# Gate sums in PSUM, bound operands on GpSimd, mask rows by DMA, and a new set of order keys

## The chip, the core and the metric

The kernel runs on one core of a Trainium2 chip. A core has a matrix engine (PE, or TensorE), a vector engine (DVE, or VectorE), a scalar engine (ACT, or ScalarE), GpSimd (POOL), and SyncE (SP), which here only issues transfers. They share an on-chip memory, SBUF; matmul results land in PSUM, eight banks of 512 float32 columns by 128 partitions. Each engine runs its own instructions in program order and waits on semaphores for the others. The metric is the device time in microseconds.

## The reference

The inputs are q, k and v for 4 batches of 8 heads, 768 positions, 64 numbers each, and three weights.

First comes an attention that selects keys. Keys are cut into 24 chunks of 32. For every query and chunk an upper bound of the dot product is formed from the chunk's smallest and largest key in each dimension:

```
ub = sum over d of max(q * k_min, q * k_max)
```

Of the chunks not in the future, the six with the largest bound are kept; scores outside them, or later than the query, are set to -1e9; softmax and the product with v follow.

Then the heads are put side by side (512 channels, x), and a gated unit follows: a causal convolution of five taps along the sequence for each channel, a sigmoid of it as the gate, `val = x @ w_val`, and `out = (gate * val) @ w_out`.

## The kernel before

**Tiling.** Heads are taken in 16 pairs, so that 128 partitions hold two heads of 64 dimensions. A pair passes through four steps, and the steps of neighbouring pairs overlap:

1. `kq`: loads of k, q and v (three buffers each) are issued on SP. PE transposes k and q into PSUM (L524), ScalarE copies them out (L535, L557) and makes a clipped copy of q (L562). VectorE reduces the keys to the largest and smallest of each chunk (L541), and `bounds` turns these into the operand KB by one subtraction of 128x24 (L574) and two of 64x48 (L581). GpSimd writes the float16 operands: KE from k (L549), QU from q (L568), VA from v (L603).
2. `sel`: PE forms the bounds in float32 (L631). VectorE adds the causal fill (L638), finds the eight largest of each row (L647) and writes NS, a one for each chunk that isn't selected (L654). PE transposes NS (L664), and 24 rows of the result are copied into the spare partitions of QU for each head: VectorE does it for the first head, ScalarE for the second (L678). The rows meet a constant of -240 in KE, so the score matmul itself adds the mask.
3. `attn`: score matmuls (L751) into eleven banks per pair, exponentials on ScalarE (L758), triangular cuts on GpSimd (L765), products with v (L782) that also give the row sums, then a reciprocal (L708) and a multiplication (L712) on VectorE. A transposing DMA (L724) writes the result into xT, where channels are on partitions.
4. `moe_gate`: the five taps of a channel tile. The first `taps` of them (`PTAPS`) are matmuls with diagonal matrices, a high and a low float16 part each (L825); the diagonals are built on VectorE in `moe_diag` (L915). The rest are multiply-adds on VectorE (L802): one for each half of the sequence, from PSUM into the float32 SBUF tile g, and then, in place in g, the others over all 768 columns. Tanh follows over 768 columns (L813). For the last two tiles of the last batch PE takes three and five taps, and all goes by halves.

When four pairs (a batch) are through, `moe_val` (L858) and its multiplication with the gate (L865), and `moe_out` (L874, copied out at L880 or L884 and stored at L887) follow.

**What sets the order.** Nothing is issued at once. Each step is added to a `Plan` with an engine, a key, a cost and the names that it reads and writes. `Plan.order` then runs a list schedule: for each engine it takes, of the operations that could start earliest, the one with the smallest key, and allots the PSUM banks under the limits `CAPS` ("w": 4 for transposes, bounds, gates and the rest, "s": 4 for scores, "av": 2). A key is the pair's number plus a small offset, for instance `p + 0.1` for `sel(p + 1)`. Where PE would rest, the planner puts in filler matmuls on zeros (L506); a block of these (L483, L506) also opens the program. The instructions on each engine follow that list, so on SP a load, a transposing DMA and a store stand in one queue.

Of the kernel before, what the change touches and what calls it, by code (L numbers as in the profile page):

```python
# [10 lines left out]
F16 = mybir.dt.float16  # L11
AF = mybir.ActivationFunctionType
# [3 lines left out]

class Op:
    __slots__ = ("eng", "key", "cost", "fn", "kind", "reads", "writes", "new", "need", "ndep",
                 "outs", "after", "ready", "end", "num", "seen")


class Plan:
# [8 lines left out]

    NBANK = 8

    def __init__(self):
        self.ops = []
        self.writer = {}
        self.readers = {}
        self.maker = {}

    def add(self, eng, key, cost, fn, r=(), w=(), new=(), kind=None, at=0.0):  # L40
        o = Op()
        o.eng, o.key, o.cost, o.fn, o.kind, o.new = eng, key, cost, fn, kind, new
# [34 lines left out]
    def order(self, bufs, caps, filler):  # L77

        users, tags, used = {}, {}, {}
        made = {}
        banks = [None] * self.NBANK
# [204 lines left out]
def kernel(  # L288
# [33 lines left out]
    X0 = XP - (KSZ - 1)  # L322
    MASKS = ("DVE", "ACT")

    PTAPS = {(b, ct): 1 + ct % 2 for b in range(B) for ct in range(NCT)}
    PTAPS[B - 1, NCT - 2] = 3
    PTAPS[B - 1, NCT - 1] = 5
    DTAPS = [max(PTAPS[b, ct] for b in range(B)) for ct in range(NCT)]
# [6 lines left out]
    for it in range(1, NT):  # L335
        for p in range(128):
# [8 lines left out]
    BUFS = {"kn": 3, "qn": 3, "vn": 3, "P5": 2, "kmx": 2, "kmr": 2,  # L345
            "q32": 2, "k32": 2, "rq": 2, "mub": 2, "top8": 2, "onat": 2, "rcp": 2, "osb": 4}
    for bi in range(11):
        BUFS[f"P{bi}"] = 2
    for ct in range(NCT):
# [25 lines left out]

    PB = [ps.tile([128, 512], FP, tag=f"bank{i}", name=f"bank{i}") for i in range(Plan.NBANK)]

    plan = Plan()
    T = {}
    new_tile = {}  # L380

# [133 lines left out]
    def kq(p, key):  # L515
# [55 lines left out]

        def bounds(ws, k0):
            c0, c1 = 12 * ws[0], 12 * ws[-1] + 12
            dve(k0, 0.2 if len(ws) > 1 else 0.16, lambda: nc.vector.tensor_tensor(  # L574
                out=T["kmr", p][:, 0, c0:c1], in0=T["kmx", p][:, c0:c1],
                in1=T["kmr", p][:, 1, c0:c1], op=ALU.subtract),
                r=[("kmx", p), ("kmr", p)] + [(x, p, w) for x in ("kmx", "kmn") for w in ws],
                w=[("kmrr", p, w) for w in ws], kind="2")
            for hh in range(2):
                hp, b0 = HP[hh], CC[hh] * NCH  # L580
                dve(k0, 0.33 if len(ws) > 1 else 0.25, lambda hp=hp, b0=b0: nc.vector.tensor_tensor(  # L581
                    out=kb[hp, :, b0 + c0:b0 + c1], in0=T["kmr", p][hp, :, c0:c1],
                    in1=T["kmr", p][hp, :, 0:1].to_broadcast([64, 2, c1 - c0]),
                    op=ALU.subtract),
                    r=[("kmr", p), ("KB", i2), ("kmrr", p, 0), ("kmn", p, 0)]
                    + [("kmrr", p, w) for w in ws],
                    w=[("KBh", i2, hh, w) for w in ws], kind="2")

        if p == 0:
            khalf(0, key)  # L590
# [25 lines left out]
    def part(p, key, g, its, nch, kb, qu, ns, iN, i2):  # L616
# [57 lines left out]
                dve(key, 0.14 + n * 0.072, lambda: fn(copy=nc.vector.tensor_copy), r, w)  # L674

        ws = (g,) if len(its) < SELT else (0, 1)
        for hh in range(2):
            mask(key + 0.35, hh, lambda hh=hh, copy=None: copy(  # L678
                out=qu[CP[hh], hh, its[0] * 128:its[0] * 128 + n * 128],
                in_=T[pt][CP[hh], :]),  # L680
                r=[pt] + [(pt, i) for i in range(n)], w=[("QM", iN, hh, w) for w in ws])
# [14 lines left out]
    def attn(p, key):  # L696
# [98 lines left out]
    def moe_gate(b, ct, key):  # L795
        slot = (b % 2) * NCT + ct
        g, taps = ("g", b, ct), PTAPS[b, ct]
        late = b == B - 1 and ct >= NCT - 2

        def tap(ki, c0, n, dst, src, k0, r, w):  # L800
            i = ki * NCT + ct
            dve(k0, 0.13 + n / 910, lambda: nc.vector.scalar_tensor_tensor(  # L802
                out=dst(), in0=xT[:, slot, X0 + c0 + ki:X0 + c0 + ki + n], scalar=cwT[:, i:i + 1],
                in1=src(), op0=ALU.mult, op1=ALU.add), r=r, w=w,
                new=new(g, f"g{ct}", [128, S]) if ki == taps and c0 == 0 else (),
                kind=None if ki == taps else "2")
            plan.also((g,))

        def half(w):
            return T[g][:, w * HB:(w + 1) * HB]  # L810

        def tanh(k0, n, dst, src, r, w, nw=()):
            act(k0, 0.11 + n / 1220, lambda: nc.scalar.activation(  # L813
                out=dst(), in_=src(), func=AF.Tanh, scale=0.5), r=r, w=w, new=nw)
            plan.also((g,))


        for w in range(2):
            pg = ("pg", b, ct, w)
            rx = [("xT", slot, x) for x in range(w + 1)]  # L820
            n = 0
            for ki in range(taps):
                for hl in range(2):
                    pe(key + 0.1 * w, HB, lambda ki=ki, hl=hl, n=n, w=w, pg=pg:
                       nc.tensor.matmul(  # L825
                           out=T[pg], lhsT=diag[ct][:, ki, hl, :],
                           rhs=xT[:, slot, X0 + w * HB + ki:X0 + w * HB + ki + HB],
# [4 lines left out]
            if taps == KSZ:  # L832
                tanh(key + 0.1 * w, HB, lambda w=w: half(w), lambda pg=pg: T[pg],
                     (pg, (pg, "o")), ((g, "t", w),),
                     new(g, f"g{ct}", [128, S]) if w == 0 else ())
                continue
            tap(taps, w * HB, HB, lambda w=w: half(w), lambda pg=pg: T[pg], key + 0.1 * w,
                rx + [pg, (pg, "o"), "cwT"], ((g, w),))
            if late:
                for ki in range(taps + 1, KSZ):  # L840
                    tap(ki, w * HB, HB, lambda w=w: half(w), lambda w=w: half(w),
                        key + 0.15 + 0.1 * w, rx + ["cwT"], ((g, w),))
                tanh(key + 0.2 + 0.1 * w, HB, lambda w=w: half(w), lambda w=w: half(w),
                     ((g, w),), ((g, "t", w),))
        if not late and taps < KSZ:
            rx = [("xT", slot, x) for x in range(2)]
            for ki in range(taps + 1, KSZ):
# [148 lines left out]
```

## Time and profile before

| | |
|---|---|
| median of three runs | 217.6 us (217.26 to 220.84) |
| the profiled execution | 219.25 us, span 217.5 us |
| PE busy | 199.2 us |
| VectorE busy | 178.0 us |
| ScalarE busy | 159.2 us |
| GpSimd busy | 135.7 us |
| DMA moved | 29.86 MB, mean 137 GB/s |

The span is the time from the first to the last instruction on the core. A group of instructions is given as: line, engine, operation, output and input, shapes, count, then busy time in us, mean duration of one in ns, and the idle time just in front of them with what ended it. Busy time joins overlapping instructions, so it can be less than count times mean. A matmul's duration includes its latency; the chain of work that ended last shows the smaller distance at which they follow each other. Waits are given as the waiting line, what it waited for, the total in us, the number of times and the longest. Filler matmuls count as busy.

### The profile page before, as it was taken

Reading aid. Unit: us, or ns where it says so; the run is one execution under the profiler, and the core shown is the slowest. Engines: PE = TensorE matmul, PEld = TensorE weight load, DVE = VectorE, ACT = ScalarE, POOL = GpSimd, SP = SyncE. Lnnn points to the kernel's source line nnn. Section 1 sums busy time; section 2 is a strip of 40 time slices with the busy share of each in tenths; the row PEclk is TensorE's granted clock in tenths of the full one; section 3 lists DMA queues with packets and bytes.
Section 4 is the critical chain, followed back from the end, with each engine's and each line's share of the span. In section 5 each row is a group of like instructions: output and inputs, shape, how many; then the busy total and the mean of one; then the engine's idle time right before and its main releaser. Section 6 shows DMA issues by size and latency. Waiting matters only on the chain.

```text
span 217.5 us, 6024 instructions
## 1 busy us (share of the span) xinstructions
PE 199.2 (92%) x2197; PEld 155.6 (72%) x2197; DVE 178.0 (82%) x527; ACT 159.2 (73%) x332; POOL 135.7 (62%) x240
## 2 busy tenths in 40 slices
PE   7989768999597997999998989999999899999993
PEld 2458657999386786878796859787978688665551
DVE  5066999697979999988899999999799999983351
ACT  0245864998398958889999669889996797888222
POOL 2069993979748898867788857677679654230000
PEclk9999996999999999999999999999999999999999
DMA  6999992999996909387898439553040100242133
GB/s 151 219 218 218 217 219 53 174 205 223 167 164 142 213 5 215 69 190 198 201 248 182 86 83 173 121 160 108 31 133 3 33 6 0 72 148 78 71 148 145
DMA packets 92268, 29.86 MB, mean 137 GB/s; under 512 B 87802, under 2 KB 89166, under 8 KB 92238
## 3 DMA queue, kind: packets, MB, share of 16 engines
q1 hardware_dynamic: 89214, 27.74, 59.8%
q0 software_dynamic: 1056, 1.05, 3.4%
q10 hardware_dynamic: 1968, 0.68, 1.5%
q8 instruction: 17, 0.28, 0.6%
q14 instruction: 13, 0.11, 0.2%
HBM read 21.27 MB, written 6.29 MB: 127 GB/s over the span
## 4 chain that ended last, share of the span: by engine, by line
PE 73%; DVE 13%; ACT 6%; issue 2%; POOL 2%; DMA 1%; POOLq 0%; ACTq 0%
PE bank L751 15%; PE bank L631 12%; PE bank L874 9%; PE bank L782 8%; PE bank L825 8%; PE bank L858 6%; PE bank L524 5%; PE bank L506 5%; DVE diag L915 3%; PE bank L483 2%; ACT QU L678 2%; DVE t_g L802 2%; DVE t_top L647 2%; PE bank L664 2%; DMA xT<-t_onat 1%
## 5 line engine op out<-in xcount | busy, mean ns | idle before, releaser
L758 ACT ACTIVATE t_P<-bank 128x512 f16<-128x512 f32 (+1 forms) x176 | 89.7, 596 | 6.9 <-PE bank L751 6.5
L751 PE MATMUL bank<-QU,KE 128*128 128x128 f16 (+4 forms) x448 | 62.5, 249 | 3.9 <-ACT QU L678 3.7
L765 POOL TENSOR_SCALAR_AFFINE_SELECT t_P<-t_P 128x384 f16<-128x384 f16 x64 | 41.3, 664 | 32.9 <-ACT t_P L758 32.6
L751 PEld LDWEIGHTS <-KE 88*128 88x128 f16 (+1 forms) x448 | 38.6, 109 | 11.2 <-issue 5.3
L549 POOL CAST KE<-t_k 64x384 f16<-64x384 f32 x64 | 36.0, 566 | 16.3 <-ACT t_k L535 11.0
L568 POOL CAST QU<-t_q 64x384 f16<-64x384 f32 x64 | 35.1, 548 | 5.6 <-ACT t_q L557 3.4
L802 DVE SCALAR_TENSOR_TENSOR t_g<-xT,cwT,t_g 128x768 f32<-128x768 f16 (+1 forms) x37 | 38.3, 1034 | 0.4
L782 PEld LDWEIGHTS <-t_P 128*128 128x128 f16 x672 | 30.7, 100 | 7.5 <-ACT t_P L758 1.8
L782 PE MATMUL bank<-VA,t_P 128*128 128x65 f16 x672 | 35.0, 195 | 0.9 <-DVE t_mub L638 0.5
L825 PE MATMUL bank<-xT,diag 128*128 128x384 f16 x116 | 28.5, 326 | 1.4 <-DMA xT<-t_onat 1.3
L631 PEld LDWEIGHTS bank<-KB,t_rq 128*128 128x128 f32 x160 | 26.5, 191 | 3.9 <-ACT t_rq L562 1.4
L631 PE MATMUL bank<-KB,t_rq 128*128 128x48 f32 (+1 forms) x160 | 27.1, 251 | 1.8 <-ACT t_k L535 0.9
L858 PE MATMUL bank<-xT,wval_sb 128*128 128x384 f16 x128 | 27.9, 326 | 0.0
L631 PE MATMUL bank<-KB,t_q 128*128 128x48 f32 (+1 forms) x160 | 27.3, 252 | 0.0
L631 PEld LDWEIGHTS bank<-KB,t_q 128*128 128x128 f32 x160 | 26.5, 191 | 0.1
L874 PE MATMUL bank<-wout_sb,t_gv 128*128 128x512 f16 x96 | 25.7, 379 | 0.0
L541 DVE TENSOR_REDUCE t_kmx<-t_k 128x12 f32<-128x384 f32 x32 | 17.2, 542 | 9.9 <-ACT t_k L535 9.7
L535 ACT ACTIVATE t_k<-bank 128x384 f32<-128x384 f32 x32 | 15.9, 516 | 9.4 <-PE bank L524 7.4
L865 DVE SCALAR_TENSOR_TENSOR t_gv<-t_g,bank 128x384 f16<-128x384 f32 x32 | 17.2, 543 | 5.2 <-PE bank L858 4.6
L880 ACT ACTIVATE t_osb<-bank 128x512 f32<-128x512 f32 x22 | 13.1, 618 | 8.8 <-PE bank L874 8.8
L557 ACT ACTIVATE t_q<-bank 128x384 f32<-128x384 f32 x32 | 16.3, 509 | 4.2 <-PE bank L524 4.1
L802 DVE SCALAR_TENSOR_TENSOR t_g<-xT,cwT,bank 128x384 f32<-128x384 f16 x30 | 18.1, 606 | 1.5 <-PE bank L825 0.8
(54 smaller groups left out, 307.5 us busy)
## 6 DMA issues: line engine op xcount, KB each, us to landing
t_vn<-in_v_dram SPq DMA_DIRECT2D x32, 192.0 KB, 4.0
out_dram<-t_osb SPq DMA_DIRECT2D x24, 256.0 KB, 2.3
t_kn<-in_k_dram SPq DMA_DIRECT2D x30, 192.0 KB, 4.2
t_qn<-in_q_dram SPq DMA_DIRECT2D x30, 192.0 KB, 4.4
wval_sb<-in_moe_w_val_dram POOLq DMA_DIRECT2D x1, 512.0 KB, 8.0
wout_sb<-in_moe_w_out_dram POOLq DMA_DIRECT2D x1, 512.0 KB, 7.8
xT<-t_onat SPq DMA_TRANSPOSE x15, 3.0
t_kn<-in_k_dram SPq DMA_DIRECT2D x2, 96.0 KB, 3.3
```

The source lines that it names most:

```text
L541: dve(k0, 0.47, lambda x=x, op_=op_: nc.vector.tensor_reduce(out=T["kmx", p][:, cs] if x == "kmx" else T["kmr", p][:, 1, cs], in_=T["k32", ...
L549: pool(k0 + (0.6 if p else 2.5), 0.56, lambda hh=hh: nc.gpsimd.tensor_copy(out=ke[HP[hh], hh, sl], in_=T["k32", p][HP[hh], sl]), r=(("k32" ...
L568: pool(k0 + 0.3, 0.56, lambda hh=hh: nc.gpsimd.tensor_copy(out=qu[HP[hh], hh, sl], in_=T["q32", p][HP[hh], sl]), r=(("q32", p, w), ("q32", ...
L631: pe(key, 48, lambda it=it, ts=ts, j=j, x=x: nc.tensor.matmul(out=cols(T[pu][:, it - 1 - i0, :]), lhsT=T[x, p][:, ts], rhs=cols(kb[:, j, : ...
L751: pe(kk, m, lambda hh=hh, c=c, jt=jt, q0=q0, m=m, bank=bank: nc.tensor.matmul(out=T[bank][:, c:c + m], lhsT=ke[KP[hh], hh, jt * 128:(jt + ...
L758: nc.scalar.activation(out=T[pt][:, 0:width], in_=T[bank][:, 0:width], func=AF.Exp, scale=0.125),
L765: nc.gpsimd.affine_select(out=ap, in_=ap, pattern=[[0, tris], [1, 128]], compare_op=ALU.is_ge, fill=0.0, base=0, channel_multiplier=-1)
L782: nc.tensor.matmul(out=T[pav][:, o0:o0 + D + 1], lhsT=T[pt][:, col:col + 128], rhs=va[:, hh, jt, :], start=st, stop=sp_, skip_group_check= ...
L802: dve(k0, 0.13 + n / 910, lambda: nc.vector.scalar_tensor_tensor(out=dst(), in0=xT[:, slot, X0 + c0 + ki:X0 + c0 + ki + n], scalar=cwT[:, ...
L825: nc.tensor.matmul(out=T[pg], lhsT=diag[ct][:, ki, hl, :], rhs=xT[:, slot, X0 + w * HB + ki:X0 + w * HB + ki + HB], start=(n == 0), stop=( ...
L858: pe(key, HB, lambda ct=ct: nc.tensor.matmul(out=T[pv], lhsT=wval_sb[:, ct, et * 128:(et + 1) * 128], rhs=xT[:, slot0 + ct, XP + w * HB:XP ...
L874: pe(key, DM, lambda et=et: nc.tensor.matmul(out=T[po], lhsT=T["gv", b, et][:, s * 128:(s + 1) * 128], rhs=wout_sb[:, et, :], start=(et == ...
```

## The change

Four things change in the computation's steps:

- **Gate sums stay in PSUM.** PE takes one tap in every ordinary gate (before: one on even channel tiles, two on odd ones; the last two tiles keep three and five). The remaining taps are multiply-adds by halves that read the PSUM bank and write it again, and tanh reads PSUM by halves and writes g.
- **Bound operands on GpSimd.** For pairs from the third on, the three subtractions of `bounds` are issued on GpSimd.
- **Mask rows by DMA.** For pairs from the third on, ScalarE copies the whole transposed selection (128 rows, 640 columns) to an SBUF tile m16, and two DMAs on SP copy 24 rows of it into QU for each head.
- **Order keys.** A table `SHIFT` adds an offset to the key of every kind of step, by engine and name, and to each of the eleven score banks. The limit "w" goes from 4 to 5. The planner's own rules and costs of the other steps stay.

```diff
+        key = round(key + self.shift.get(eng + ":" + what, 0.0), 4)
...
+    MDMA = 2
+    KBPOOL = True
+
-    PTAPS = {(b, ct): 1 + ct % 2 for b in range(B) for ct in range(NCT)}
+    PTAPS = {(b, ct): 1 for b in range(B) for ct in range(NCT)}
     PTAPS[B - 1, NCT - 2] = 3
     PTAPS[B - 1, NCT - 1] = 5
...
-    CAPS = {"w": 4, "s": 4, "av": 2, "spare": 2}
+    SHIFT = {
+        "SP:kn": -0.2, "ACTQ:kn": -3.6, "SP:qn": 0.7, "ACTQ:E00": -0.6, "SP:vn": -0.62,
+        "SP:cwn": -4.1, "DVE:KB": -1.2, "POOL:NS": 4.8, "POOL:VA": 1.2, "DVE:diag1": 3.8,
+        "DVE:diag": 3.6, "PE:knT": -1.9, "ACT:k32": -2.0, "DVE:kmx": 1.8, "DVE:kmn": 1.6,
+        "POOL:KE": -0.8, "DVE:KBh": 2.8, "PE:qnT": -1.88, "ACT:q32": -0.4, "ACT:rq": -0.2,
+        "POOL:QU": -7.4, "DVE:top8": -2.0, "DVE:NS": -4.0, "PE:sT": -0.6, "POOL:kmrr": -1.2,
+        "POOL:KBh": -4.6, "PE:s": 0.36, "bank0": 0.67, "ACT:P": 0.15, "POOL:Ptri": 0.3,
+        "PE:av": -1.2, "bank1": 0.53, "DVE:rcp": -2.5, "DVE:onat": -1.8, "bank3": -0.2,
+        "bank4": -0.06, "bank5": -0.04, "bank6": -0.55, "bank7": 0.1, "bank8": 0.12,
+        "bank9": -0.62, "bank10": -0.24, "PE:pg": 1.23, "ACT:m16": -4.6, "PE:pv": 0.4,
+        "DVE:gv": -3.4, "PE:po": 0.35, "ACT:osb": 1.5, "PE:xTp": 0.9,
+    }
+    CAPS = {"w": 5, "s": 4, "av": 2, "spare": 2}
...
         def bounds(ws, k0):
+            onp = KBPOOL and p > 1
+            eng = nc.gpsimd if onp else nc.vector
...
+        if p >= MDMA:
+            act(key + 0.35, 0.14 + n * 0.0915, lambda: nc.scalar.copy(out=T["m16", p], in_=T[pt]),
+                r=[pt] + [(pt, i) for i in range(n)], w=(("m16", p),),
+                new=new(("m16", p), "m16", [128, SELT * 128], F16))
+            for hh in range(2):
+                sp(key + 0.35, 60, lambda hh=hh: nc.sync.dma_start(
+                    out=qu[CP[hh], hh, 128:S], in_=T["m16", p][CP[hh], :]),
+                    r=(("m16", p),), w=[("QM", iN, hh, w) for w in ws])
+            return
...
-            kk = key + 0.085 * n
+            kk = key + 0.085 * n + SHIFT.get(f"bank{n}", 0.0)
...
-        if not late and taps < KSZ:
-            rx = [("xT", slot, x) for x in range(2)]
-            for ki in range(taps + 1, KSZ):
-                tap(ki, 0, S, lambda: T[g], lambda: T[g], key + 0.2, rx + ["cwT"],
-                    ((g, 0), (g, 1)))
-            tanh(key + 0.3, S, lambda: T[g], lambda: T[g], ((g, 0), (g, 1)),
-                 ((g, "t", 0), (g, "t", 1)))
+            for ki in range(taps, KSZ):
+                i, c0 = ki * NCT + ct, X0 + w * HB + ki
+                dve(kk, 0.525, lambda pg=pg, i=i, c0=c0: nc.vector.scalar_tensor_tensor(
+                    out=T[pg], in0=xT[:, slot, c0:c0 + HB], scalar=cwT[:, i:i + 1],
+                    in1=T[pg], op0=ALU.mult, op1=ALU.add),
+                    r=rx + [pg, "cwT"], w=((pg, "o"),))
+            act(kk + 0.05, 0.385, lambda w=w, pg=pg: nc.scalar.activation(
+                out=T[g][:, w * HB:(w + 1) * HB], in_=T[pg], func=AF.Tanh, scale=0.5),
+                r=(pg, (pg, "o")), w=((g, "t", w),),
+                new=new(g, f"g{ct}", [128, S]) if w == 0 else ())
```

Among the orders that follow from it: all diagonals are now built ahead of the first pair's selection, VectorE's first work of that kind waits for the transposed convolution weights, and on SP the first loads of v stand ahead of the first of q.

More of the change, by code (lines that the diff above doesn't have):

```diff
@@ L18, with __init__ @@
     __slots__ = ("eng", "key", "cost", "fn", "kind", "reads", "writes", "new", "need", "ndep",
-                 "outs", "after", "ready", "end", "num", "seen")
+                 "outs", "after", "ready", "end", "num", "at")
 class Plan:
     NBANK = 8
-    def __init__(self):
+    def __init__(self, shift):
+        self.shift = shift
         self.ops = []
@@ L41, in add @@
         o = Op()
-        o.eng, o.key, o.cost, o.fn, o.kind, o.new = eng, key, cost, fn, kind, new
+        what = w[0]
+        while isinstance(what, tuple):
+            what = what[0]
+        if isinstance(w[0], tuple) and w[0][-1] == "tri":
+            what = what + "tri"
+        key = round(key + self.shift.get(eng + ":" + what, 0.0), 4)
+        o.eng, o.key, o.cost, o.fn, o.kind, o.new, o.at = eng, key, cost, fn, kind, new, at
         o.reads, o.writes = tuple(r), tuple(w)
@@ L77, in order @@
     def order(self, bufs, caps, filler):
+        self.args = caps, bufs
         users, tags, used = {}, {}, {}
@@ L342 @@
     cfill_dr = nc.inline_tensor(cfill_np, name="cfill")
-    CAPS = {"w": 4, "s": 4, "av": 2, "spare": 2}
+    SHIFT = {
[11 more added lines that the diff above has]
+    CAPS = {"w": 5, "s": 4, "av": 2, "spare": 2}
     BUFS = {"kn": 3, "qn": 3, "vn": 3, "P5": 2, "kmx": 2, "kmr": 2,
-            "q32": 2, "k32": 2, "rq": 2, "mub": 2, "top8": 2, "onat": 2, "rcp": 2, "osb": 4}
+            "q32": 2, "k32": 2, "rq": 2, "mub": 2, "top8": 2, "onat": 2, "rcp": 2, "osb": 4, "m16": 2}
     for bi in range(11):
@@ L376 @@
     PB = [ps.tile([128, 512], FP, tag=f"bank{i}", name=f"bank{i}") for i in range(Plan.NBANK)]
-    plan = Plan()
+    plan = Plan(SHIFT)
     T = {}
@@ L573, in bounds, with tt @@
             c0, c1 = 12 * ws[0], 12 * ws[-1] + 12
-            dve(k0, 0.2 if len(ws) > 1 else 0.16, lambda: nc.vector.tensor_tensor(
+            onp = KBPOOL and p > 1
+            eng = nc.gpsimd if onp else nc.vector
+            def tt(cost, *args, **kw):
+                if onp:
+                    pool(k0, cost, *args, **kw)
+                else:
+                    dve(k0, cost, *args, **kw, kind="2")
+            tt(0.2 if len(ws) > 1 else 0.16, lambda: eng.tensor_tensor(
                 out=T["kmr", p][:, 0, c0:c1], in0=T["kmx", p][:, c0:c1],
@@ L577, in bounds @@
                 r=[("kmx", p), ("kmr", p)] + [(x, p, w) for x in ("kmx", "kmn") for w in ws],
-                w=[("kmrr", p, w) for w in ws], kind="2")
+                w=[("kmrr", p, w) for w in ws])
             for hh in range(2):
                 hp, b0 = HP[hh], CC[hh] * NCH
-                dve(k0, 0.33 if len(ws) > 1 else 0.25, lambda hp=hp, b0=b0: nc.vector.tensor_tensor(
+                tt(0.33 if len(ws) > 1 else 0.25, lambda hp=hp, b0=b0: eng.tensor_tensor(
                     out=kb[hp, :, b0 + c0:b0 + c1], in0=T["kmr", p][hp, :, c0:c1],
@@ L586, in bounds @@
                     + [("kmrr", p, w) for w in ws],
-                    w=[("KBh", i2, hh, w) for w in ws], kind="2")
+                    w=[("KBh", i2, hh, w) for w in ws])
         if p == 0:
@@ L797, in moe_gate @@
         g, taps = ("g", b, ct), PTAPS[b, ct]
[L798 to L815, printed above, removed]
         for w in range(2):
-            pg = ("pg", b, ct, w)
+            pg, kk = ("pg", b, ct, w), key + 0.1 * w
             rx = [("xT", slot, x) for x in range(w + 1)]
@@ L823, in moe_gate @@
                 for hl in range(2):
-                    pe(key + 0.1 * w, HB, lambda ki=ki, hl=hl, n=n, w=w, pg=pg:
+                    pe(kk, HB, lambda ki=ki, hl=hl, n=n, w=w, pg=pg:
                        nc.tensor.matmul(
@@ L831, in moe_gate @@
                     n += 1
[L832 to L839, printed above, removed]
-                for ki in range(taps + 1, KSZ):
[L841 to L844, printed above, removed]
-        if not late and taps < KSZ:
-            rx = [("xT", slot, x) for x in range(2)]
-            for ki in range(taps + 1, KSZ):
-                tap(ki, 0, S, lambda: T[g], lambda: T[g], key + 0.2, rx + ["cwT"],
-                    ((g, 0), (g, 1)))
-            tanh(key + 0.3, S, lambda: T[g], lambda: T[g], ((g, 0), (g, 1)),
-                 ((g, "t", 0), (g, "t", 1)))
+            for ki in range(taps, KSZ):
[8 more added lines that the diff above has]
+                new=new(g, f"g{ct}", [128, S]) if w == 0 else ())
+            plan.also((g,))
     def moe_val(b, et, w, key):
```

## The prediction

> **What bounds the kernel now.** I read the page first: the busy shares, the forty slices, the chain.
>
> ```profile
> PE 199.2 (92%) x2197; PEld 155.6 (72%) x2197; DVE 178.0 (82%) x527; ACT 159.2 (73%) x332; POOL 135.7 (62%) x240
> PE   7989768999597997999998989999999899999993
> PEclk9999996999999999999999999999999999999999
> PE 73%; DVE 13%; ACT 6%; issue 2%; POOL 2%; DMA 1%; POOLq 0%; ACTq 0%
> ```
>
> The matrix engine carries 73% of the chain; 27%, some 58 us, is spent on others. One slice, the seventh (32.6 to 38.1 us), has a lowered clock, and the slices in front of it hold PE's longest rest. So next I cut the chain and the waits there. In the chain the columns are start, time, what:
>
> ```profile
> 29.50 0.46 DVE t_kmr L541
> 29.96 1.61 DVE diag L915 x5
> ...
> 32.18 0.77 DVE t_top L647 x10
> ...
> 33.13 0.41 DVE NS L654
> ...
> 33.58 0.45 PE bank L664 x5
> ```
>
> ```profile
> PE bank L664 <- DVE NS L654: 3.0, 1, 3.0
> ```
>
> VectorE is building the diagonal matrices (L915) while the second pair's selection waits behind them; PE rests 3.0 us (30.57 to 33.58), and the windows of one microsecond show the clock at 0.67, 0.50, 0.50 and 0.62 from 34 to 38 us. After 36 us the wait list, limited to 36 to 214 us, gives the selection again:
>
> ```profile
> PE bank L751 <- ACT QU L678: 3.3, 6, 0.9
> PE bank L664 <- DVE NS L654: 1.6, 2, 1.1
> ```
>
> These two are 4.9 of the 8.5 us that PE rests between 36 and 204 us (busy 159.5 of 168.0 in the windows). VectorE is busy 147.9 of those 168.0 (88%), so it is the second bound.
>
> **What it is made of, part by part.** The groups, with shapes kept apart, price most of it:
>
> ```profile
> L802 DVE SCALAR_TENSOR_TENSOR t_g<-xT,cwT,t_g 128x768 f32<-128x768 f16 x35 | 37.0, 1058 | 0.3
> L802 DVE SCALAR_TENSOR_TENSOR t_g<-xT,cwT,bank 128x384 f32<-128x384 f16 x30 | 18.1, 606 | 1.5 <-PE bank L825 0.8 <-ACT t_g L813 0.3 <-ACT t_P L758 0.2
> L813 ACT ACTIVATE t_g<-t_g 128x768 f32<-128x768 f32 x14 | 12.0, 858 | 4.9 <-DVE t_g L802 4.9
> L678 ACT COPY QU<-bank 24x640 f16<-24x640 f16 x15 | 10.2, 682 | 8.6 <-PE bank L664 8.0 <-DVE QU L678 0.4
> L581 DVE TENSOR_TENSOR KB<-t_kmr 64x48 f32<-64x48 f32 x30 | 8.1, 271 | 0.4
> L678 DVE COPY QU<-bank 24x640 f16<-24x640 f16 x15 | 7.3, 489 | 2.2 <-PE bank L664 1.4 <-ACT QU L678 0.3
> L574 DVE TENSOR_TENSOR t_kmr<-t_kmx,t_kmr 128x24 f32<-128x24 f32 x15 | 5.3, 355 | 0.0
> ```
>
> *Gate matmuls.* One tap instead of two on the odd channel tiles of every ordinary gate: the new program has 88 such matmuls for 116. The chain passes four in 0.65 us, 0.163 each: 28 x 0.163 = 4.6 us less, on PE's own path. **-4.6.**
>
> *Taps in PSUM.* 35 full-width taps, 30 half-width and two late halves go; 116 half-width ones come, each reading and writing a PSUM bank. Start to start, a full tap takes about 1.02 us, a half one that reads PSUM 0.52 (78.88 to 79.40), when an independent instruction follows: 35 x 1.02 + 32 x 0.52 = 52.3 us. In the new order 24 of the taps stand right behind the one that they depend on, so they cost the whole 0.61: 92 x 0.52 + 24 x 0.61 = 62.5, **10 us more**. The Trainium skill (VectorE: DVE Perf Modes, rules for kernel authors) speaks against this edit: where many operations follow on a matmul's output, copy it to SBUF first. Its cycle table (same page, the errata section) has 120 cycles of overhead from PSUM for 58 in SBUF, 65 ns per operation, or 7.5 us on 116. The rows answer otherwise: half of a full SBUF tap is 0.51, a PSUM one 0.52; the full SBUF taps run up to 1.32 us, while the PSUM form stays within 0.593 to 0.615. I take the rows. No row shows VectorE writing PSUM: from nothing to another 65 ns, so 0 to 7.5 us; I take 0, since reading PSUM showed nothing either.
>
> *Bound operands.* 28 of L581 and 14 of L574 leave VectorE: start to start about 0.2 and 0.3, so 28 x 0.2 + 14 x 0.3 = 9.8 us there. *Mask copies.* VectorE loses 14 of L678 at 0.45: 6.3. *Diagonals.* two fewer, 0.7. With the taps: 62.5 - 52.3 - 9.8 - 6.3 - 0.7 = -6.6 us. Besides, the new order puts all diagonals at the start; some eight now stand after 35.4 us, at 0.37 each (15 in 5.56 us of the chain) 3.0. The crowded stage thus loses 9.6 us of VectorE work. The part of that which reaches the end lies between its share of the chain (28 of 178 us, 16%: 1.5) and all of it; I take **-3**, near the lower end, as PE follows close.
>
> *GpSimd* gets those 42 small operations. It has no two-input row; its nearest is the 64x384 cast, 0.55, which caps them at 23 us; by length alone (48 of 384) they would be 0.2 or so, 8 us. The Trainium skill (GPSIMD Engine Reference, engine selection) is against such moves, two-input elementwise work being about twice as slow: 2 x 0.27 x 28 + 2 x 0.355 x 14 = 25 us. GpSimd rests 82 us, 32.6 of it in front of the triangular select for the exponentials. Covered, so 0; without cover three operations of at most 0.56 delay each pair's bounds by 1.7.
>
> *ScalarE*: 14 copies of 128 rows for 14 of 24 rows, 640 long both (0: time goes by length); 32 half-width tanh at 0.49 (the half form from PSUM) for 14 at 0.86 plus four at 0.5: +1.6 us. It rests 27 us in 36 to 204. 0.
>
> *Masks by DMA.* Per pair a ScalarE copy of 0.68, two issues on SP at 0.5 each (as the first loads), and a landing of 2.0 to 2.3 (the 64 KB identity and the 256 KB outputs; these are 30 KB): 3.7 to 4.2 us, where a copy took 0.7. Behind them on SP queue loads, transposes and stores. The new order pays for it: taking PE's list at the chain's rates, between a pair's mask transposes and its first score matmul lie 5.7 to 12.2 us of other PE work, for 0 to 1.1 before. So the copies' and selections' rests of 4.9 us should go, and I give back 0.9: **-4**.
>
> *The start.* The new PE list reaches the conv-weight transpose at 13.2 us: 8.65 (the warm-up's end), 19 fillers at 0.215, a few transposes. VectorE's list waits for that first, then: three small steps to 14.1, four key reductions at 0.46 to 16.0, eight diagonals at 0.37 and the bounds to 19.9, twelve more diagonals to 24.3, then the sums, maxima, two reductions and the selection, to 26. First scores then come at about 27.5 for 18.8 now. PE would rest over 4 us in there; the rest of 3.0 was followed by the half clock for 3.4 us, which costs 1.7. To the second pair's scores the list has 9.6 us of PE work: 27.5 + 9.6 + 1.7 = 38.8, for 35.4 now: +3.4, say **+3.6** with a wait. If the diagonals run at 0.17, as the quickest do (23.51 to 23.68), it is 4 us less, -0.4; a second slow spell would make it 5. GpSimd is casting beside them, as it is beside the 15, so I take 3.6. In exchange the present slow spell, 2.4 us of it after 35.4, goes: **-1.2**.
>
> **Sum**: -4.6 - 3 - 4 + 3.6 - 1.2 = -9.2 us. The profiled execution took 219.25 with a span of 217.5; the median of the runs shown, 217.6, lies by the span, so I subtract from the median: 208.4.
>
> **The rivals.** *VectorE becomes the bound.* If a tap that writes PSUM costs 0.67 whatever follows (0.606 and 65 ns), 116 are 77.7, not 62.5: VectorE's crowded stage has 147.9 - 9.6 + 15.2 = 153.5 us. At 94% busy (its ten-microsecond windows from 110 to 190 us average 9.4) that stage takes 163.3, 4.7 less than now, and with the start's +3.6 the whole is 216.5. For it: 88% busy now; against: PSUM reads cost nothing visible. It also holds each gate's bank for some 2.6 us (four taps and a tanh) for 0.6, with five banks allowed for such work.
>
> *The mask arrives late* (the slower side). Place: SP's queue, in front of each pair's first scores. The profile of that queue shows waits of up to 12.6 us for the attention output and 7.1 for a value buffer; a mask transfer behind one of these waits too. The lead is 1.5 to 8 us over its path. Fourteen pairs share it: every microsecond by which the mean mask misses its lead is 14 us, so 0.66 us uses up the gain, and from 0.97 the kernel is over 2% slower; at 1.1, 224. Against: the order moves the loads along too.
>
> *The start is not won back*, the other rests being replaced: +3.6 - 4.6 and nothing else, 216.6. *The order does more*: VectorE's 9.6 count in full, -6.6 more: 202.
>
> That the edits don't happen is excluded: the instruction lists of the new program show them.
>
> **Numbers.** Chances: forecast 0.56, VectorE bound 0.13, start not won back 0.10, late masks 0.10, order does more 0.11. The range of 203 to 217 holds the forecast with its unknowns (0 to 7.5 for the PSUM writes, -0.4 to 5 for the start) and most of the cases on either side. The measurement tells 2% (4.4 us) from no change: faster than 213.2 0.71, within 0.18, slower 0.11.
>
> **What would show it.** Right: 88 gate matmuls; no rest of PE at 30 us but one near 22 to 26, with a slow-clock slice; first scores past 24 us; PSUM taps near 0.6; the waits of L751 for the mask gone; VectorE under 173 us busy. Wrong: score matmuls that wait for a DMA, taps over 0.65, a VectorE above 92% from 40 to 190, or first scores before 21.

## The result and the profile after

The changed kernel takes **204.33 us** (median of four runs, 203.08 to 204.57), against 217.43 us (217.0 to 220.84) of the kernel before, run beside it. The ratio is 0.939 with a 95% interval of 0.935 to 0.943, so it is faster by 13.1 us. The forecast was 208.4, the range 203 to 217. The profiled execution took 204.38 us with a span of 202.7, 14.8 less than the span before. In the experiments below a ratio compares undisturbed runs alone, while a median takes in all runs of a kernel; no_keys_five had too few undisturbed ones for a ratio.

The page of the kernel after: busy shares, two rows of the forty slices (a digit is PE's busy share or its granted clock in tenths), and the chain by engine.

```profile
PE 192.2 (95%) x2140; PEld 153.7 (76%) x2140; DVE 167.8 (83%) x518; ACT 158.9 (78%) x346; POOL 127.8 (63%) x282
...
PE   7998489999999999999999999999999999999992
...
PEclk9999757999999999999999999999999999999999
...
PE 85%; ACT 7%; DVE 2%; DMA 2%; issue 1%; POOL 1%; ACTq 0%
```

From the seventh slice (30.4 us) to the second last, PE's row holds nothing but nines. The part of the chain that isn't PE's fell from 27% of 217.5 us (58.7) to 15% of 202.7 (30.4). A new dent is in slice 5, and a lowered clock in slices 5 to 7.

The windows of the kernel after. The columns are busy time of PE, PE's weight loads, VectorE, ScalarE and GpSimd with their counts, then the granted clock, the DMA share and GB/s.

```profile
20.00:25.00 5.00, 2.41 (x17) 2.07 (x16) 4.80 (x19) 1.81 (x6) 1.61 (x4) 0.79 1.03 195
25.00:30.00 5.00, 4.23 (x26) 3.36 (x26) 2.68 (x12) 3.22 (x7) 3.44 (x7) 0.50 1.22 230
30.00:35.00 5.00, 5.00 (x42) 4.57 (x40) 1.36 (x4) 3.97 (x9) 2.33 (x7) 0.69 0.52 91
...
36.00:190.00 154.00, 152.84 (x1898) 129.01 (x1898) 143.93 (x441) 141.55 (x311) 107.19 (x239) 1.00 0.66 146
```

Between 36 and 190 us PE rests 1.2 of 154 us; before, it rested 8.5 in the same window (145.5 busy). VectorE is busy 143.9 of 154, 93.5%, where it was 140.8. And from 23 to 33 us PE ran at half clock.

What PE waits for in the kernel after, from 36 to 190 us. These two lines are the whole answer.

```profile
PE bank L824 <- ACT t_P L800: 0.4, 1, 0.4
PE bank L793 <- DVE bank L859: 0.3, 1, 0.3
```

The mask waits (3.3 us) and selection waits (1.6) of before are gone. Nor does any line here name a DMA. At the start the largest wait is this one:

```profile
PE bank L697 <- DVE NS L687: 2.6, 1, 2.6
```

The chain in those microseconds, kernel after (start, time, what):

```profile
14.99 3.73 DMA t_vn<-in_v_dram
18.73 3.16 DVE diag L931 x11
21.89 0.12 DVE t_mub L671
22.04 0.38 DVE t_top L680 x4
...
23.33 0.13 DVE NS L687
...
23.50 0.40 PE bank L697 x2
```

The twenty diagonals run on VectorE from 15.1 to 21.9 us, the first pair's selection stands behind them, and PE rests from 20.9 to 23.5 us. The first scores come at 25.3 us (before: 18.8).

The groups of the kernel after, shapes kept apart:

```profile
L850 PE MATMUL bank<-xT,diag 128*128 128x384 f16 x88 | 22.3, 326 | 0.0
...
L859 DVE SCALAR_TENSOR_TENSOR bank<-xT,cwT,bank 128x384 f32<-128x384 f16 x116 | 70.9, 616 | 4.3 <-PE bank L850 3.4
...
L807 POOL TENSOR_SCALAR_AFFINE_SELECT t_P<-t_P 128x384 f16<-128x384 f16 x64 | 32.9, 524 | 15.0 <-ACT t_P L800 13.2
L614 POOL TENSOR_TENSOR KB<-t_kmr 64x48 f32<-64x48 f32 x28 | 7.5, 267 | 0.8
L607 POOL TENSOR_TENSOR t_kmr<-t_kmx,t_kmr 128x24 f32<-128x24 f32 x14 | 3.4, 242 | 2.0 <-DVE t_kmx L565 1.2
```

A tap that reads and writes PSUM takes 616 ns, one that only read PSUM took 606: the write costs 10 ns, 1.2 us on 116. VectorE's total fell from 178.0 to 167.8. GpSimd's fell too, from 135.7 to 127.8, although it got 42 operations (10.9 us) more: its triangular selects, untouched by the change, went from 664 to 524 ns. The same gate matmuls and selects in the kernel before:

```profile
L825 PE MATMUL bank<-xT,diag 128*128 128x384 f16 x116 | 28.5, 326 | 1.4 <-DMA xT<-t_onat 1.3
...
L765 POOL TENSOR_SCALAR_AFFINE_SELECT t_P<-t_P 128x384 f16<-128x384 f16 x64 | 41.3, 664 | 32.9 <-ACT t_P L758 32.6
```

### The profile page after: what moved, and what is told of

Its sections match the earlier page's. It is cut to its first block, busy times and chain, and to the rows that moved or that the text cites. A ratio compares the mean times of both kernels' runs of the same rounds, so it can differ in the third digit from the quotient of the medians.

```text
span 202.7 us, 6045 instructions
## 1 busy us (share of the span) xinstructions
PE 192.2 (95%) x2140; PEld 153.7 (76%) x2140; DVE 167.8 (83%) x518; ACT 158.9 (78%) x346; POOL 127.8 (63%) x282
## 4 chain that ended last, share of the span: by engine, by line
PE 85%; ACT 7%; DVE 2%; DMA 2%; issue 1%; POOL 1%; ACTq 0%
PE bank L793 17%; PE bank L664 13%; PE bank L890 10%; PE bank L874 10%; PE bank L548 10%; PE bank L824 10%; PE bank L850 7%; PE bank L530 4%; ACT t_P L800 4%; PE bank L507 2%; PE bank L697 2%; DMA t_vn<-in_v_dram 2%; DVE diag L931 2%; ACT t_k L559 1%; POOL KE L573 1%
## 5 line engine op out<-in xcount | busy, mean ns | idle before, releaser
L800 ACT ACTIVATE t_P<-bank 128x512 f16<-128x512 f32 (+1 forms) x176 | 92.8, 614 | 2.1 <-PE bank L793 1.6
L859 DVE SCALAR_TENSOR_TENSOR bank<-xT,cwT,bank 128x384 f32<-128x384 f16 x116 | 70.9, 616 | 4.3 <-PE bank L850 3.4
L592 POOL CAST QU<-t_q 64x384 f16<-64x384 f32 x64 | 32.0, 504 | 24.3 <-PE bank L793 15.6
L807 POOL TENSOR_SCALAR_AFFINE_SELECT t_P<-t_P 128x384 f16<-128x384 f16 x64 | 32.9, 524 | 15.0 <-ACT t_P L800 13.2
L573 POOL CAST KE<-t_k 64x384 f16<-64x384 f32 x64 | 32.4, 514 | 8.7 <-ACT t_k L559 5.4
L824 PE MATMUL bank<-VA,t_P 128*128 128x65 f16 x672 | 33.9, 193 | 0.4 <-ACT t_P L800 0.4
L664 PEld LDWEIGHTS bank<-KB,t_rq 128*128 128x128 f32 x160 | 27.5, 194 | 2.3 <-ACT t_q L581 0.9
L890 PE MATMUL bank<-wout_sb,t_gv 128*128 128x512 f16 x96 | 28.4, 379 | 0.0
L565 DVE TENSOR_REDUCE t_kmr<-t_k 128x12 f32<-128x384 f32 x32 | 17.4, 545 | 7.7 <-ACT t_k L559 7.7
L559 ACT ACTIVATE t_k<-bank 128x384 f32<-128x384 f32 x32 | 16.5, 516 | 8.1 <-PE bank L548 7.7
L850 PE MATMUL bank<-xT,diag 128*128 128x384 f16 x88 | 22.3, 326 | 0.0
L863 ACT ACTIVATE t_g<-bank 128x384 f32<-128x384 f32 x32 | 16.5, 518 | 5.0 <-DVE bank L859 2.9
```

What stands on the lines that cost most here:

```text
L573: pool(k0 + (0.6 if p else 2.5), 0.56, lambda hh=hh: nc.gpsimd.tensor_copy(out=ke[HP[hh], hh, sl], in_=T["k32", p][HP[hh], sl]), r=(("k32" ...
L592: pool(k0 + 0.3, 0.56, lambda hh=hh: nc.gpsimd.tensor_copy(out=qu[HP[hh], hh, sl], in_=T["q32", p][HP[hh], sl]), r=(("q32", p, w), ("q32", ...
L664: pe(key, 48, lambda it=it, ts=ts, j=j, x=x: nc.tensor.matmul(out=cols(T[pu][:, it - 1 - i0, :]), lhsT=T[x, p][:, ts], rhs=cols(kb[:, j, : ...
L800: nc.scalar.activation(out=T[pt][:, 0:width], in_=T[bank][:, 0:width], func=AF.Exp, scale=0.125),
L807: nc.gpsimd.affine_select(out=ap, in_=ap, pattern=[[0, tris], [1, 128]], compare_op=ALU.is_ge, fill=0.0, base=0, channel_multiplier=-1)
L824: nc.tensor.matmul(out=T[pav][:, o0:o0 + D + 1], lhsT=T[pt][:, col:col + 128], rhs=va[:, hh, jt, :], start=st, stop=sp_, skip_group_check= ...
```

## The experiments

Besides the change, twelve kernels were run, each beside the kernel before. Ratios are to that one.

| run | what differs | median us | ratio (95%) |
|---|---|---|---|
| after | the change | 204.33 | 0.939 (0.935 to 0.943) |
| no_keys | edits, no offsets, 4 banks | 216.47 | 0.995 (0.990 to 1.000) |
| no_keys_five | edits, no offsets, 5 banks | 214.83 | - |
| no_keys_copy | no_keys, masks copied | 216.66 | 0.994 (0.989 to 0.999) |
| caps_four | the change with 4 banks | 208.15 | 0.956 (0.950 to 0.962) |
| keys_only | before, offsets, 5 banks | 234.0 | 1.074 (1.065 to 1.083) |
| bounds_dve | after's order, bounds on VectorE | 212.18 | 0.972 (0.965 to 0.979) |
| mask_copy | after's order, masks copied | 212.13 | 0.965 (0.955 to 0.975) |
| mask_twice | after's order, one more DMA per mask | 226.7 | 1.036 (1.026 to 1.046) |
| taps_sbuf | after's order, gate sums in SBUF | 215.03 | 0.983 (0.972 to 0.993) |
| taps_two | after's order, 12 taps back on PE | 207.2 | 0.945 (0.936 to 0.955) |
| diag_late | after, 12 diagonals later | 199.9 | 0.917 (0.909 to 0.925) |
| keys_a | diag_late with offsets found anew | 202.89 | 0.925 (0.917 to 0.933) |

The theory was the prediction's: each edit takes some work off a path, and the order gives the masks their lead. The rivals were that the edits carry the gain and the offsets don't matter, that the offsets carry it alone, and that neither does without the other.

### The edits without the offsets, the offsets without the edits

```diff
-    SHIFT = { ... }
-    CAPS = {"w": 5, "s": 4, "av": 2, "spare": 2}
+    SHIFT = {}
+    CAPS = {"w": 4, "s": 4, "av": 2, "spare": 2}
```

> The three edits of the computation stay (gate taps in PSUM, bound operands on GpSimd, masks by DMA); the table of key offsets is emptied and the limit of working banks is 4 again. Theory A (the new order carries most of the gain, because it lets each pair's selection run several microseconds ahead of its scores): 213 to 219 us, with mask transfers that now stand on the path: score matmuls waiting for the mask again, over 5 us of rests on PE after the start. Theory B (the relief of PE and VectorE by the edits carries it): 204 to 209 us.

Measured: 216.47 us. The kernel before was 217.49 beside it. no_keys, chain by engine:

```profile
PE 57%; DVE 19%; ACT 12%; DMA 7%; issue 2%; POOL 0%; SPq 0%; ACTq 0%; POOLq 0%; DVEq 0%
```

and its waits of PE:

```profile
PE bank L686 <- DVE NS L676: 4.3, 4, 2.7
PE bank L782 <- DMA QU<-t_m: 2.2, 2, 1.1
```

VectorE is busy 171.6 us here, so the edits do relieve it by 6.4 (the forecast had 6.6), and yet hardly anything comes of it: PE still rests 8.1 us between 36 and 190, as before. Of the two expectations the first holds, that the order carries most of the gain; but the mask transfers it named are a small part of the rests (2.2 us).

The other way round, the kernel before got the same `SHIFT` and five banks.

> The kernel before with only the new key offsets and the limit of 5 working banks; no edit of the computation. Theory A: most of the gain is here, 206 to 211 us. Theory B: 214 us or more, since PE has the 28 gate matmuls back and VectorE its copies and subtractions. A third reading (offsets fit only the operations that they were found for): slower than 218 us.

Measured: 234.0 us, 16.5 more than before: the third reading of the three. The waits of PE and three windows of keys_only:

```profile
PE bank L650 <- DVE KB L600: 3.6, 1, 3.6
```

```profile
154.00:156.00 2.00, 0.00 (x0) 0.00 (x0) 2.00 (x4) 0.84 (x1) 0.00 (x0) 1.00 0.99 265
...
158.00:160.00 2.00, 2.00 (x11) 2.00 (x11) 1.11 (x2) 0.00 (x0) 0.00 (x0) 0.50 0.05 18
```

```profile
170.00:175.00 5.00, 5.00 (x41) 4.81 (x40) 1.82 (x14) 2.92 (x6) 2.21 (x5) 0.50 0.00 0
```

VectorE is fully busy with other work while PE rests 3.6 us for the bounds' operand, the longest of its waits here; then PE runs at half clock from 157 to 181 us though it is nearly always busy. Summing over one-microsecond windows PE's busy time times the missing share of the clock gives 14.3 us in this execution and 1.7 in that of the kernel before: 12.6 of the 17.2 us by which the span grew. (The sum is an upper estimate; in after it gives 4.4, where a comparison further down finds 3.0.)

So the edits alone give 1.0, the offsets with the fifth bank lose 16.5, and all together gain 13.1. The offsets were found for the edits' costs, and on the kernel before they lose. The gain can't be split into shares of single parts.

### The fifth bank

```diff
-    CAPS = {"w": 5, "s": 4, "av": 2, "spare": 2}
+    CAPS = {"w": 4, "s": 4, "av": 2, "spare": 2}
```

> The changed kernel with the limit for transposes, bounds and gates back at four banks, its offsets kept; the whole computation is there. A gate now holds its bank for some 2.6 us. Theory A, the fifth bank is what the gates in PSUM need and carries a good part of the gain: 209 us or more, with PE waiting for VectorE's taps or for the tanh in front of a bank. Theory B, the offsets carry it and the fifth bank is a small help: 203.5 to 207.

> The edits without the offsets (216.5 us with four banks), with the limit at five banks. Theory A, the fifth bank carries a good part of the gain: 208 to 212. Theory B, the offsets do: 214 to 218. The leads of the masks stay at 2.8 to 6.4 us, against 5.7 to 12.7 with the offsets.

Measured: 208.15 and 214.83 us. The first lies between the two expectations, the second in the offsets' own. With the edits in place the fifth bank is worth 1.6 us without offsets (212.55 to 216.6 against 215.26 to 218.42, so hardly more than the scatter) and 3.8 with them; the offsets are worth 8.3 with four banks and 10.5 with five. Offsets carry most of it. By these medians both together give 2.2 us more than their sum, which the scatter of no_keys_five does not allow to be called shown.

### Taking back one edit in the order of after

The next four keep the order of after on every engine, and change only what the steps issue. Their PE list is the same, 2140 matmuls, so a stretch of it can be compared: the time from the start of the 401st matmul to the start of the 2096th, and PE's rests within it, both from the starts and ends in the trace. The table has the three that ran it at full clock, as after did.

| | stretch us | rest | busy | start of the 401st |
|---|---|---|---|---|
| after | 140.3 | 1.2 | 139.2 | 49.6 |
| bounds_dve | 146.4 | 3.8 | 142.5 | 51.3 |
| mask_copy | 149.9 | 7.2 | 142.8 | 46.3 |
| taps_sbuf | 151.4 | 7.4 | 144.0 | 49.4 |

**Bounds.**

```diff
-            eng = nc.gpsimd if onp else nc.vector
+            eng = nc.vector
```

so the 42 operations stand in VectorE's list at the places where GpSimd had them.

> The changed kernel in its own order; the 42 bound subtractions are issued on VectorE at the places where GpSimd had them. If VectorE (143.9 of 154 us busy in the middle stage) is a bound beside PE, its 10 us more come out at the end for the greater part: 209 to 214 us. If the order leaves it room: 203 to 206.

Measured: 212.18, 7.9 us more than after, for 11.3 us more of VectorE work (179.1). Of these 7.6 us fall in the stretch, which grew by 6.0. bounds_dve, a wait of PE and a group:

```profile
PE bank L664 <- DVE KB L614: 2.1, 3, 1.2
```

```profile
L614 DVE TENSOR_TENSOR KB<-t_kmr 64x48 f32<-64x48 f32 x30 | 9.6, 320 | 0.3
```

On VectorE the recorded duration of a subtraction is 320 ns here, on GpSimd it was 267; the last section has the distance at which they follow each other, which says otherwise.

**Masks.** The same places of the list now hold a copy by VectorE and one by ScalarE, and no DMA.

```diff
-            act(..., lambda: nc.scalar.copy(out=T["m16", p], in_=T[pt]), ...
+            act(..., lambda: (
+                nc.vector.tensor_copy(out=qu[CP[0], 0, 128:S], in_=T[pt][CP[0], :]),
+                nc.scalar.copy(out=qu[CP[1], 1, 128:S], in_=T[pt][CP[1], :])), ...
```

> The changed kernel in its own order; the 14 masks are copied from PSUM straight into the operand, by VectorE for the first head and ScalarE for the second, where ScalarE made its copy; the 28 mask transfers go. If the edit is worth the VectorE time that it frees (14 x 0.45 = 6.3 us): 206 to 210 us. If it is worth nothing once the order is found, or costs through its transfers: 201 to 205.

Measured: 212.13, 7.8 more than after and over both expectations, for 9.1 us more of VectorE (176.9). That median is the middle of two pairs of runs: 210.4 and 210.5 at full clock, 213.8 and 214.1 at a mean clock of 0.976. Against after's two at 0.975 (204.4 and 204.6) the second pair lost 9.5 us, and the stretch, at full clock in both kernels, is 9.6 us longer. mask_copy, chain by engine and two waits of PE:

```profile
PE 49%; DVE 33%; ACT 11%; issue 5%; POOL 1%; DVEq 0%; ACTq 0%
```

```profile
PE bank L851 <- ACT QU L713: 2.3, 5, 0.6
PE bank L875 <- ACT QU L713: 1.6, 2, 1.0
```

These waits, 3.9 us, are for a bank that the copies hold, so not all of the loss is VectorE's time: it is busy 8.3 us more in the stretch. VectorE's share of the chain is 33% for 2%.

**Gate sums.** The 86 taps behind the first write a half of g in SBUF, and tanh reads it there; the order and the sizes stay.

```diff
-                    out=T[pg], in0=xT[:, slot, c0:c0 + HB], scalar=cwT[:, i:i + 1],
-                    in1=T[pg], op0=ALU.mult, op1=ALU.add),
+                    out=gh, in0=xT[:, slot, c0:c0 + HB], scalar=cwT[:, i:i + 1],
+                    in1=T[pg] if ki == taps else gh, op0=ALU.mult, op1=ALU.add)
...
```

> The changed kernel in its own order; each gate's first multiply-add writes an SBUF tile and the further ones work in place there by halves, as before the change (that was over the whole width), and tanh reads SBUF. Same number of instructions. If PSUM costs VectorE time: taps under 0.55 us each and the time falls to 198 to 202. If instructions with two SBUF inputs and GpSimd's stand in each other's way: taps of over 0.64 on average with a wide spread, GpSimd's casts back from 0.51 to 0.55 us and its triangular selects from 0.52 to over 0.6, and 206 to 212 us.

Measured: 215.03, 10.7 more than after, the contention of the second expectation and more than its 206 to 212. taps_sbuf, four groups and a wait of PE:

```profile
L863 DVE SCALAR_TENSOR_TENSOR t_g<-xT,cwT,t_g 128x384 f32<-128x384 f16 x86 | 61.8, 720 | 0.8
...
L807 POOL TENSOR_SCALAR_AFFINE_SELECT t_P<-t_P 128x384 f16<-128x384 f16 x64 | 37.3, 594 | 12.7 <-ACT t_P L800 11.1 <-POOL KE L573 0.3
...
L863 DVE SCALAR_TENSOR_TENSOR t_g<-xT,cwT,bank 128x384 f32<-128x384 f16 x30 | 18.2, 606 | 3.2 <-PE bank L850 2.4 <-ACT t_g L869 0.6
...
L614 POOL TENSOR_TENSOR KB<-t_kmr 64x48 f32<-64x48 f32 x28 | 10.4, 370 | 0.8
```

```profile
PE bank L824 <- POOL t_P L807: 4.3, 9, 0.8
```

Both engines slow down together: a tap 720 ns for 616, a select 594 for 524, a subtraction on GpSimd 370 for 267. GpSimd's busy time grows by 21.0 us to 148.8, and PE waits for its cuts. Only the place of the sums differs between the two kernels. Within this trace the slowing follows the overlap: the ten SBUF taps with GpSimd at rest took 610 ns, the 69 with GpSimd busy over half of their time 743; selects took 682 ns when an SBUF tap covered over half of them and 532 with none beside them. In after a tap takes 616 either way. And the first tap of each gate here, which reads PSUM and writes SBUF, stays at 606. So the SBUF form is no slower by itself, and what freed GpSimd is that the taps no longer have both operands in SBUF. The Trainium skill names the cause (GPSIMD Engine Reference, section 1, Specifications): GpSimd shares its SBUF interfaces with VectorE, and VectorE instructions with two SBUF inputs contend with it.

**One more DMA per mask.** Each mask goes through a second SBUF tile.

```diff
-                sp(..., nc.sync.dma_start(out=qu[CP[hh], hh, 128:S], in_=T["m16", p][CP[hh], :]),
+                    if hh == 0:
+                        nc.sync.dma_start(out=T["m16b", p], in_=T["m16", p])
+                    nc.sync.dma_start(out=qu[CP[hh], hh, 128:S], in_=T["m16b", p][CP[hh], :])
```

> The changed kernel in its own order; each mask passes through a second SBUF tile, by one more transfer that the two others wait for, so its way is some 2.5 us longer and SP's queue stands as long. If the lead of the selection (5.7 to 12.7 us of PE work for a way of 4 us) is what hides the transfers: within 2 us of the changed kernel, 203.5 to 206.5, with waits of score matmuls for the mask under 3 us. If the masks are only just in time: 14 x 1 us or more, 212 to 235.

Measured: 226.7, 22.4 more than after, far above what the lead's theory expected and inside the other's 212 to 235. mask_twice, a wait of SP's queue and two of PE:

```profile
SPq L720 <- DMA t_m16b<-t_m: 35.2, 14, 6.1
```

```profile
PE bank L880 <- DMA xT<-t_onat: 9.1, 2, 4.9
PE bank L799 <- DMA QU<-t_m16b: 4.8, 3, 2.3
```

The masks themselves are late three times. Most of the wait is the transposing DMAs' of the attention output, which stand behind the masks on SP while SP waits 2.5 us for each extra landing. The half clock after such rests adds 9.9 us by the sum used above (4.4 in after). So the masks themselves mostly stay in time, by their lead, but SP's queue has no room for a wait: the late-mask rival named the right place, with the victim behind it on the queue.

### Is PE the bound?

In six gates (channel tiles 2 and 3 of the first three batches) PE takes a second tap: two matmuls more for each half, 24 in all, and VectorE has 12 half-width taps fewer.

```diff
+                        if last and more:
+                            for h2 in range(2):
+                                nc.tensor.matmul(out=T[pg], lhsT=diag[ct][:, 1, h2, :], ...
...
```

> The changed kernel in its own order, but the gates of the two last channel tiles in the first three batches take a second tap on PE again, right behind the first (24 more gate matmuls, 12 multiply-adds fewer on VectorE). If PE is the bound and the gate matmuls are worth what the chain says (0.163 us each): +3.9 us, 207.5 to 209. If VectorE is the bound: 12 x 0.52 = 6 us less there, so the time falls to 199 to 203. Both bounds even: within 1.5 us of the changed kernel.

Measured: 207.2 (204.88 to 208.64), just under the first reading's range and 2.9 more than after, for 24 x 0.163 = 3.9 us more matmuls and 4.9 us less VectorE (162.9). By the medians PE's work counts for about 0.7 of its length, with a scatter wider than for the others. The traces are clearer: both kernels reach the 401st matmul at 49.5 to 49.6 us, and from there the stretch with the 24 more in it takes 144.3 us for 140.3, so these count in full although VectorE got less. Less work on VectorE buys nothing in this order, and more costs most of its length (bounds_dve): PE is the bound, with VectorE right behind it.

### The masks without the lead

no_keys with the masks copied out of PSUM in place of the transfers (`MDMA = 16`).

> The gate sums and the bound operands of the change kept, the offsets emptied, five banks back to four, and the mask rows copied out of PSUM by VectorE and ScalarE as before, for every pair; nothing is left out of the computation. In the version with the mask transfers and no offsets the lead of a pair's mask over its first scores was 2.6 to 7.2 us for a path of about 4; with the copies the list gives 0.1 to 3.3, as before the change. Theory A, the transfers without their lead are what ate the gain of the other two edits there: 211 to 214 us. Theory B, without the offsets a gate that sits in PSUM for four taps and the new orders of VectorE are the loss, and the transfers cost nothing: 216.5 or more, since VectorE gets about 6 us of copies back.

Measured: 216.66 against no_keys' 216.47. That is the second expectation: the transfers cost nothing there and save nothing. Copies add 6.8 us of VectorE work (178.4) without effect, and PE waits 3.6 us for copies where it waited 2.2 for transfers. So these microseconds of VectorE's are worth nothing without the offsets, while in the order of after more of them cost 0.8 us each (6.0 for 7.6 in bounds_dve's stretch).

### The start

The order builds 12 diagonals, needed only by the last two gates, in front of the first selection. Given a later earliest start in the planner, they move behind it; the order of all other instructions stays.

```diff
-                        r=("identh", "cwT", "cwl"), w=(("diag1", ct, ki, part),))
+                        r=("identh", "cwT", "cwl"), w=(("diag1", ct, ki, part),),
+                        at=22.0 if ki else 0.0)
```

> The changed kernel with one thing moved: the twelve diagonals that PE first needs in the last batch are built behind the first pair's selection, not in front of it; the order of all other instructions is the same. If these diagonals are what delays the start: PE's rest of 2.6 us in front of the first mask transposes goes to under 0.5, the half-clock spell of 10 us does not come or is shorter than 4 us, first scores 3 us earlier, and the whole takes 196 to 201 us. If the start is held by the transfers of the first loads, or the time is taken back later because VectorE is full: 203 to 205 us, no change.

Measured: **199.9 us** (199.07 to 201.92), 4.4 less than after, the fastest kernel here. diag_late, two rows of the slices and the wait of before:

```profile
PE   7998988999999999999999999999999999999992
...
PEclk9999999999999999999999999999999999999999
```

```profile
PE bank L697 <- DVE NS L687: 0.3, 1, 0.3
```

The first scores come at 22.4 us for 25.3, the rest of 2.6 us is 0.3, and there is no half clock. The stretch from the 401st to the 2096th matmul takes 140.3 us as in after; the 401st starts at 45.0 for 49.6. mask_copy has the order of after's start and the same rest of 2.6 us, but ran at full clock: from the end of that rest to the 401st matmul it takes 23.1 us, after 26.1. So about 3.0 us of the 4.6 are the half clock's, 1.6 the earlier work's. That is one execution of each; two of after's four runs had a mean clock of 0.992 and two 0.975, with times within 0.3 us in three of them, so how much of the 4.4 in the medians is the clock's stays open.

Last, the offsets were found anew on the schedule's model with 0.33 us for a diagonal in place of 0.16.

> The version with the twelve late diagonals held back, with the planner's cost of a diagonal set to 0.33 us (what they take beside GpSimd's casts) in place of 0.16 and the offsets found anew for that; all of the change's edits kept, and nothing left out of the computation. The leads of the masks stay at 4.3 to 12.1 us. Theory A, offsets carry over when they come from the same planner and costs near the measured ones: 198 to 201 us, no matter the one kernel for the other, since PE already has the whole middle. Theory B, offsets hold a narrow fit and a new set loses what the first had: 204 or more.

Measured: 202.89 us (200.99 to 205.29; the kernel before took 219.07 beside it), between the two expectations. Its ratio of 0.925 overlaps diag_late's interval: another set of offsets from the same planner, for the same edits, does about as well, and no better. PE rests 0.9 us between 36 and 190 us in it.

## Why the prediction was right

By span the kernel lost 14.8 us: PE's rests fell from 18.4 to 10.5 (-7.9) and its busy time from 199.2 to 192.2 (-7.0). Against the forecast's terms:

- **Gate matmuls, -4.6: right in the new order.** They number 88; their group fell from 28.5 to 22.3 us, and 24 of them put back lengthen the stretch by 4.0 us where the same price gives 3.9 (by the medians 2.9). In no_keys, with the same 28 gone, the whole gained 1.0: there PE's own path did not shorten by itself, which the term had assumed.
- **Taps in PSUM, PSUM write taken at 0: right.** 616 ns for 606. The rule that was weighed against it, to copy to SBUF first, would have been wrong by 10.7 us here (taps_sbuf), and not for the reason considered: the sum was made per instruction, and what the SBUF form costs is the contention with GpSimd. That part of the gain was in no term of the sum; the full SBUF taps of up to 1.32 us that the prediction read were its only sign.
- **Bounds on GpSimd, covered: right**, with durations of 267 and 242 ns (10.9 us, inside the 8 to 23).
- **Masks -4 and VectorE -3: right as a sum of rests, wrong as prices.** PE's rests in the middle fell by 7.3. But the step "I take -3, near the lower end, as PE follows close" failed: within this order the bounds put back on VectorE lengthen the stretch by 6.0 us for 7.6 us of work, and the mask copies by 9.6. These prices hold in this order alone and can't be added; that -4 and -3 sum up to nearly the measured rests is in part luck. (A mask's issue on SP took 0.76 us at the median for the 0.5 of the prediction, which its lead covered.) And the step behind both, that the end can be moved by the rests that the profile shows, was too small. In the stretch above, the same 1695 matmuls of the list are busy 139.2 us in after and 142.5 to 144.0 in the three kernels with an edit taken back, 3.4 to 4.8 us more. Taken matmul by matmul, nearly all of it sits in 25 to 33 of them in each kernel, 77 of these 84 waiting for a semaphore, as only one in five of all does: short waits that stand inside the busy time, since a matmul's recorded duration includes its latency. The rival "the order does more" (202) was nearest on this.
- **The start, +3.6 - 1.2: right in sign, its parts off.** First scores at 25.3 for 27.5 (the diagonals had some quick ones, 20 in 6.8 us), but a spell at half clock of 10.2 us for 3.4. Rests up to 36 us fell by 0.9, the half clock took about 3.0 where the one before was put at 1.7: together about +0.4 for +2.4.

So -4.6, -7.3 for the rests of the middle and about +0.4 for the start make -11.5. Fillers and warm-up matmuls are busy 1.9 us less (20.7 to 18.8). The other 1.4 us or so may be the short waits, which weren't measured for the kernel before itself, whose list is another. The forecast was thus right by terms that are each near the mark or offset one another: the start was put too high by 2.0 us, the rest too low. The medians moved by 13.1 only, because the profiled execution of before (219.25 us) was one of its longer ones.

**The rivals.** VectorE as the bound: it reached 93.5% from 36 to 190, over the 92% that the prediction had named as a sign against it, and PE rested only 1.2 us; so the sign was badly chosen: PE was full, and VectorE nearly. Late masks: not in after, where the score matmuls' weight loads wait 0.5 us for one transfer in all, but with one more landing the kernel falls by the predicted route to 226.7. The start not won back: it was.

## What to carry to other kernels

Count what an engine's relief is worth with the order that uses it: the edits here were worth 1 us in the old order, the new order cost 16.5 without them, and together they gave 13.1. Before moving an operation between SBUF and PSUM, look at what it does to the engine beside it: here a tap cost VectorE as much either way, and GpSimd decided. PE's rests are less than what an order can win, because short waits hide in matmul durations; compare the time of one stretch of matmuls between kernels. Look for work in front of the first use that nobody needs yet: moving 12 diagonals gave 4.4 us more.

## What the runs showed of the hardware

- VectorE operations with both operands in SBUF slow GpSimd and themselves: by 70 ns on a select of 524, by 104 on a tap of 616. With the sums in PSUM GpSimd's casts too were quicker than before, 514 for 566 and 504 for 548 ns.
- A two-input subtraction of 64x48 float32 has a recorded duration of 267 ns on GpSimd and of 271 to 320 on VectorE, but durations mislead here. Where one follows another with nothing between, they start 332 ns apart on GpSimd (median of nine pairs in after) and 206 to 209 on VectorE (four pairs in before, six in bounds_dve), a ratio of 1.6. The Trainium skill's about twofold price (GPSIMD Engine Reference, section 4.1, Engine selection) is nearly reached at this size, and the move paid because GpSimd had the time.
- The granted clock changes on a grid. In all fourteen traces the changes lie whole multiples of 3.41 us apart, and a spell at half clock lasts one (before), two, three (after) or seven (keys_only) of these steps. So it matters how a rest falls on the grid. The rest of 2.6 us in after left PE busy 42% of one step, and half clock followed; in mask_copy the same rest was divided between two steps, 58% and 67% busy, and none followed. Every step with PE busy 42% or less was followed by half clock. A step with 51% was followed by it in taps_sbuf and was not in no_keys_copy, so these runs give no sharp threshold. In after the steps inside the spell were 82 and 78% busy and the spell went on; the third, fully busy, ended it; in keys_only four fully busy ones had to follow one another. The Trainium skill's advice to keep PE's rests under about 3 us (TensorE: Matmul & The Clock Gate, Why this matters for your kernels) is not tight enough for this case.
